# First q and k as fp32 rows by the hardware queue, and an instruction order planned with new transfer rates

## The chip, the cores and the metric

One core of a Trainium2 chip (trn2). The metric is device time in microseconds (us) from the first to the last moment of one execution; medians over several executions are given with their range. A profile has a slightly shorter "span", from the first to the last instruction that it records. The kernel before takes 317.6 us.

## The reference

Sliding-window attention on 8 batches of 8 heads, 576 positions, 64 wide, then a two-layer network on the 4608 resulting tokens:

```python
scores = (1/sqrt(64)) * q @ k.T              # q, k, v: 8 x 8 x 576 x 64, fp32
mask   = (rel >= 0) & (rel < 64)             # rel = query position - key position
attn   = softmax(where(mask, scores, -1e9))
x      = (attn @ v), heads side by side      # 4608 x 512
h      = x @ w_in                            # 512 -> 2048
out    = (h * sigmoid(h)) @ w_out            # 2048 -> 512
```

## The kernel before

The kernel works on bf16 tiles in on-chip memory. Batches 0 to 3 get q (and 0 and 1 get k) by a load that casts fp32 to bf16 in flight, followed by a transpose on TensorE and a copy ("lift") out of its accumulator. Later batches load rows, also cast to bf16 on the way, and have a DMA transpose turn them. v comes in 128-row blocks; VectorE then makes a copy of it that is shifted by 64 partitions (`shift_v`). While TensorE does the two layers for earlier tokens, the attention of the next batch runs between those matmuls. Every exponentiated score tile of batches 1 to 7 is multiplied by the 0/1 mask on VectorE before TensorE may multiply it with v.

No one wrote the order of the instructions by hand. The kernel holds a list scheduler, `Plan`. Each operation is added with the engine it may use, an estimate of its time, what it depends on, and a rank. `run` then plays the whole execution through with these estimates; whenever an engine comes free, it takes the ready operation of best rank. The order that results is emitted, and is fixed from then on: on the chip each engine works through its list in order, whatever the real times are. A transfer has a planned time too:

```python
if op["dma"] is None:
    op["seen"] = end + op["lat"]
else:
    soft = e == "POOL"
    pipe[soft] = max(pipe[soft], pipe[False], end + 0.9) + op["dma"]     # one pipe per kind of queue
    op["seen"] = pipe[soft] + (2.0 if c in ("xk", "xo") else 1.4)        # when it is believed to have landed
```

The parts that the argument touches (cut):

```python
rank=dict(..., exp=1, mask=1, lift=2, spread=2, shift=2, cast=4, ...)    # plus b, the batch: smaller goes first

def load_cast(w, b, pj, kk):                  # q or k of one pair of heads, cast in flight
    nc.gpsimd.dma_start(out=natbs[w]..., in_=(q, k)[kk][b, 2 * pj:2 * pj + 2]...)

def shift_v(b, hf, a, z):                     # copies on VectorE only
    t = vv[b % NK][:, 2 * NB * a:2 * NB * z + 1, 0:D]
    if hf: nc.vector.tensor_copy(out=t[0:64, 2::2], in_=t[64:128, 1::2])
    else:  nc.vector.tensor_copy(out=t[64:128, 0:-1:2], in_=t[0:64, 1::2])

def masking(n, g):
    nc.vector.tensor_mul(es[n % NE], es[n % NE], mask0 if g == 0 else mask)

# planned times of transfers: rows of q, k in later batches 0.6; cast loads 1.0;
# v 1.3; each of the 8 pieces of w_in 1.55, of w_out 1.38
p.add("dma", {"POOL": 1.0}, lambda e, part=part: load_v(e, b, part), busy, dma=1.3)

# matmuls without a use, which fill TensorE's idle time until the first layer is well under way
p.add_filler(60, "warm", {"PE": 0.17}, warm, [*c_bias, c_ident], gate=..., pool="all")
```

The softmax here doesn't subtract the row's maximum and nothing guards it: scores larger than these inputs give would overflow.

## Time and profile before

| | before |
|---|---|
| time | 317.61 us (317.55 to 318.02, 3 runs) |
| TensorE busy | 97% of a span of 315.6 us |
| first layer's first matmul | 24.8 us |
| first transposes | 6.45 us |
| last row of v (batch 7) landed | 188.35 us |

The prediction below shows the lines that carry this. One view is added here, the waits of TensorE. Its columns are what waited, for what, the total in us, how often, and the longest:

```profile
PE at L657 <- DVE bias L191: 3.5, 1, 3.5
PE at L287 <- DMA natb<-in_q_dram: 0.6, 1, 0.6
```

L657 are the warm-up matmuls and L287 are the first transposes. Apart from the start, then, TensorE waits for nobody for longer than a few tenths.

### The profile page before, as it was taken

The page shows a single profiled execution, that of the slowest core. Times are in us where ns is not written, and L with a number is a line of the kernel's source. Part 1 is how long each engine was busy: PE and PEld are TensorE (multiplying, and loading weights), DVE is VectorE, ACT ScalarE, POOL GpSimd, SP SyncE. Part 2 cuts the span into 40 slices and gives each one's busy share as a digit, 9 for nine tenths or more (in the row PEclk, how much of TensorE's full clock was granted, in tenths as well). Part 3 has the DMA queues.
Part 4 walks back from the last instruction along what each step waited for, and adds up shares of the span by engine and source line. Part 5 has one row for each costly group of instructions (what it writes and reads, how often), then busy time and mean ns, then how long its engine had stood idle before and what let it go on. Part 6 is the DMA issues. An engine that isn't in the chain of part 4 may idle for free.

```text
span 315.6 us, 6086 instructions
## 1 busy us (share of the span) xinstructions
PE 307.6 (97%) x2231; PEld 167.7 (53%) x2231; DVE 152.8 (48%) x465; ACT 194.1 (61%) x381; POOL 120.8 (38%) x161
## 2 busy tenths in 40 slices
PE   5899999999999999999999999999999999999995
PEld 2668666545655456545654565455444444444444
DVE  5691858854788638895895089606800000000000
ACT  8798795787848687467618762777176136316611
POOL 8965958876748642867645400000000000000000
PEclk9999999999999999999999999999999999999999
DMA  7999999999999999999999995302320110020011
GB/s 68 173 194 189 158 200 167 154 226 160 144 152 158 152 95 159 200 162 132 157 162 188 167 156 119 83 1 56 95 58 2 66 66 2 18 82 33 3 66 66
DMA packets 137309, 37.03 MB, mean 117 GB/s; under 512 B 121664, under 2 KB 132800, under 8 KB 137280
## 3 DMA queue, kind: packets, MB, share of 16 engines
q0 software_dynamic: 96128, 18.36, 78.6%
q1 hardware_dynamic: 41152, 18.29, 31.1%
q8 instruction: 17, 0.28, 0.4%
q14 instruction: 12, 0.10, 0.1%
HBM read 36.70 MB, written 9.44 MB: 146 GB/s over the span
## 4 chain that ended last, share of the span: by engine, by line
PE 92%; DVE 2%; DMA 2%; ACT 1%; POOL 1%; issue 1%; POOLq 0%; ACTq 0%; DVEq 0%
PE mp L428 39%; PE mp L437 39%; PE at L363 5%; PE at L337 5%; DMA natb<-in_q_dram 2%; PE at L296 1%; PE at L419 1%; PE at L287 1%; PE at L657 0%; DVE qbd L309 0%; POOL natb L232 0%; PE mp L657 0%; ACT L355 0%; PE mp L408 0%; POOL vv L260 0%
## 5 line engine op out<-in xcount | busy, mean ns | idle before, releaser
L437 PE MATMUL mp<-w_out_sb,g 128*128 128x512 bf16 (+2 forms) x608 | 145.4, 367 | 0.0
L428 PE MATMUL mp<-bridge,w_in_sb 128*128 128x512 bf16 (+2 forms) x640 | 129.7, 358 | 0.1
L434 ACT ACTIVATE g<-mp 128x512 bf16<-128x512 f32 (+2 forms) x160 | 86.5, 555 | 30.0 <-PE mp L428 29.7
L428 PEld LDWEIGHTS <-w_in_sb 128*128 128x128 bf16 x640 | 60.4, 98 | 59.6 <-issue 0.4
L437 PEld LDWEIGHTS <-g 128*128 128x128 bf16 x608 | 54.4, 97 | 41.3
L443 ACT COPY ot<-mp 128x512 f32<-128x512 f32 (+2 forms) x36 | 20.1, 563 | 73.7 <-PE mp L437 56.8
L392 DVE TENSOR_TENSOR ox<-at,rc 64x192 bf16<-64x192 f32 x120 | 42.4, 354 | 2.6
L242 POOL DMA_DIRECT2D nat<-in_k_dram x48 | 36.1, 754 | 17.1 <-DMA vv<-in_v_dram 7.0
L260 POOL DMA_DIRECT2D vv<-in_v_dram x32 | 32.0, 1002 | 24.8 <-PE at L363 15.5
L355 ACT ACTIVATE e<-at 128x384 bf16<-128x384 f32 x89 | 37.9, 498 | 2.1 <-PE at L337 1.9
L358 DVE TENSOR_TENSOR e<-e,mask 128x384 bf16<-128x384 bf16 x84 | 26.5, 346 | 24.5 <-ACT e L355 23.8
L363 PEld LDWEIGHTS <-e 128*128 128x128 bf16 x288 | 22.6, 96 | 15.2 <-DVE e L358 2.1
L363 PE MATMUL at<-vv,e 128*128 128x130 bf16 x273 | 29.8, 219 | 0.0
L242 POOL DMA_DIRECT2D nat<-in_q_dram x32 | 24.3, 764 | 7.9 <-DMA nat<-in_q_dram 4.7
L337 PE MATMUL at<-qbd,kt 128*128 128x128 bf16 x252 | 22.8, 219 | 0.2
L337 PEld LDWEIGHTS <-kt 128*128 128x128 bf16 x252 | 17.8, 98 | 9.6 <-issue 1.4
L369 DVE RECIPROCAL rc<-at 128x6 f32<-128x6 f32 x91 | 17.3, 194 | 10.0 <-PE at L363 8.2
L302 DVE COPY qbd<-at 64x288 bf16<-64x288 bf16 x25 | 12.0, 479 | 16.0 <-ACT qbd L302 14.4
L375 DVE TENSOR_TENSOR ob<-at,rc 64x192 bf16<-64x192 f32 x48 | 16.8, 350 | 0.9
L256 DVE COPY qbd<-raw 64x1152 bf16<-64x1152 bf16 x16 | 7.9, 497 | 13.2 <-DMA raw<-nat 12.9
L302 ACT COPY qbd<-at 64x288 bf16<-64x288 bf16 x23 | 11.0, 478 | 2.9 <-DVE qbd L302 1.9
L232 POOL DMA_DIRECT2D natb<-in_q_dram x16 | 10.7, 670 | 4.8 <-PE mp L428 1.3
(66 smaller groups left out, 160.9 us busy)
## 6 DMA issues: line engine op xcount, KB each, us to landing
out_dram<-ot SPq DMA_DIRECT2D x35, 256.0 KB, 2.5
vv<-in_v_dram POOLq DMA_DIRECT2D x32, 144.0 KB, 6.9
nat<-in_k_dram POOLq DMA_DIRECT2D x48, 72.0 KB, 8.0
natb<-in_q_dram POOLq DMA_DIRECT2D x16, 144.0 KB, 6.3
nat<-in_q_dram POOLq DMA_DIRECT2D x32, 72.0 KB, 8.1
w_in_sb<-in_moe_w_in_dram POOLq DMA_DIRECT2D x8, 256.0 KB, 8.4
w_out_sb<-in_moe_w_out_dram POOLq DMA_DIRECT2D x8, 256.0 KB, 8.3
natb<-in_k_dram POOLq DMA_DIRECT2D x8, 144.0 KB, 5.9
```

The costliest lines, as they stand in the source:

```text
L242: nc.gpsimd.dma_start(out=rows(i)[:, pj % 2, :, 64 * hh:64 * hh + 64], in_=(q, k)[kk][b, 2 * pj + hh].rearrange("(m p) d -> p m d", p=NR),)
L260: queue[e].dma_start(out=vv[b % NK][:, 2 * g0 + 1:2 * g1 + 1:2, 0:D], in_=v[b].rearrange("h s d -> (h s) d").rearrange("(g p) d -> p g d", ...
L302: copies[e](out=qbd[b % NK][64 * hh:64 * hh + 64, pj, hh].rearrange("x (p m) -> x p m", m=NM)[:, :, r::2], in_=at_bf16(op)[64 * r:64 * r + ...
L337: nc.tensor.matmul(at_sp(op)[:, x], lhsT=kt[b % NK][:, pj * S + t * 64:pj * S + t * 64 + 128], rhs=qbd[b % NK][:, pj, :, t * 64:t * 64 + 6 ...
L355: nc.scalar.activation(out=es[n % NE], in_=at_sp(op), func=ACTF.Exp, scale=scale)
L358: nc.vector.tensor_mul(es[n % NE], es[n % NE], mask0 if g == 0 else mask)
L363: nc.tensor.matmul(at_pv(op)[:, x], lhsT=es[n % NE][:, x].rearrange("p h i -> p (h i)"), rhs=vv[b % NK][:, s:s + NB + 1:NB, 0:D + 1], star ...
L392: nc.vector.tensor_mul(ox(n)[:, :, r], pv[r, :, hh, 0:D], rc[r, :, hh:hh + 1].to_broadcast([64, 3, 64]))
L428: nc.tensor.matmul(banks[bank["bank"]][:, lo:hi], lhsT=w_in_sb[:, c, ft * 128:(ft + 1) * 128], rhs=bridge[:, (j * TT + lo) // 64:(j * TT + ...
L434: nc.scalar.activation(out=gts[gt][:, lo:hi], in_=banks[bank["bank"]][:, lo:hi], func=ACTF.Silu)
L437: nc.tensor.matmul(banks[bank["bank"]][:, 0:hi - lo], lhsT=gts[gt][:, m * 128:(m + 1) * 128], rhs=w_out_sb[:, f, lo:hi], start=(f == 0), s ...
L443: copies[e](out=ots[ot][:, lo:hi], in_=banks[bank["bank"]][:, 0:hi - lo])
```

## The change

The intent has two parts. (1) The first pair's q and k no longer wait behind GpSimd's cast loads: SyncE loads them as fp32 rows, and VectorE or ScalarE cast them. (2) The planned times of transfers are replaced by rates measured on batch 1 and on the weights, so that the plan resembles the chip more closely. The planned time of the identity constant is corrected along with them (0.5 to 1.3).

```diff
-    c_ident = p.add("one", {"POOL": 0.5}, const_ident)
+    c_ident = p.add("one", {"POOL": 1.3}, const_ident)
...
+    def load_first(i, kk):                      # fp32 rows, hardware queue
+        nc.sync.dma_start(out=nats[i]....bitcast(FP32)..., in_=(q, k)[kk][0, 0:2]...)
+    def cast_first(e, i, w):
+        copies[e](out=natbs[w], in_=nats[i]....bitcast(FP32))
...
+                if (b, pj) == (0, 0):
+                    ld = p.add("ld0", {"SP": 0.45 if kk else 1.2}, ... load_first(i, kk), dma=1.15)
+                    ca = [p.add("cast", {"ACT": 0.84, "DVE": 0.56}, ... cast_first(e, i, w), [ld], b=b)]
+                else:
-                ca = [p.add("dma", {"POOL": 0.66}, ... load_cast(w, b, pj, kk), ..., dma=1.0)]
+                    ca = [p.add("dma", {"POOL": 0.66}, ... load_cast(w, b, pj, kk), ..., dma=0.85 if b else 1.0)]
...
-    p.add("dma", {"POOL": 1.0}, ... load_v(e, b, part), busy, dma=1.3)
+    p.add("dma", {"POOL": 1.0}, ... load_v(e, b, part), busy, dma=1.1 if b else 1.3)
...
-    win.append(p.add("dma", {"POOL": 0.8}, ... load_w_in(f), dma=1.55))
+    win.append(p.add("dma", {"POOL": 0.8}, ... load_w_in(f), dma=1.35))
...
-    wout.append(p.add("dma", {"POOL": 0.8}, ... load_w_out(f), dma=1.38))
+    wout.append(p.add("dma", {"POOL": 0.8}, ... load_w_out(f), dma=1.28))
```

The four `dma=` edits change no transfer. They change only what the planner believes, and through that the order of everything.

More of the change, by code (lines that the diff above doesn't have):

```diff
@@ L235, in load_cast @@
         )
+    def load_first(i, kk):
+        nc.sync.dma_start(
+            out=nats[i].rearrange("p j m x -> p (j m x)").bitcast(FP32).rearrange("p (h y) -> p h y", h=2),
+            in_=(q, k)[kk][0, 0:2].rearrange("h (p m) d -> p h (m d)", m=NM),
+        )
+    def cast_first(e, i, w):
+        copies[e](out=natbs[w], in_=nats[i].rearrange("p j m x -> p (j m x)").bitcast(FP32))
     def rows(i):
@@ L507, in add_batch_qk @@
                 n_nat[1] += 1
-                ca = [p.add("dma", {"POOL": 0.66}, lambda _, w=w, pj=pj, kk=kk: load_cast(w, b, pj, kk),
-                            [natb_free.get(w)] + (v_landed[b - 1] if b > 2 else []), dma=1.0)]
+                if (b, pj) == (0, 0):
+                    i = n_nat[0] % NN
+                    n_nat[0] += 1
+                    ld = p.add("ld0", {"SP": 0.45 if kk else 1.2}, lambda _, i=i, kk=kk: load_first(i, kk), dma=1.15)
+                    ca = [p.add("cast", {"ACT": 0.84, "DVE": 0.56}, lambda e, i=i, w=w: cast_first(e, i, w), [ld], b=b)]
+                    nat_free[i] = ca[0]
+                else:
+                    ca = [p.add("dma", {"POOL": 0.66}, lambda _, w=w, pj=pj, kk=kk: load_cast(w, b, pj, kk),
+                                [natb_free.get(w)] + (v_landed[b - 1] if b > 2 else []), dma=0.85 if b else 1.0)]
                 by = {"ACT": 0.64, "DVE": 0.75}
@@ L535, in add_v_loads @@
         v_landed.setdefault(b, []).extend(
-            p.add("dma", {"POOL": 1.0}, lambda e, part=part: load_v(e, b, part), busy, dma=1.3) for part in parts)
+            p.add("dma", {"POOL": 1.0}, lambda e, part=part: load_v(e, b, part), busy, dma=1.1 if b else 1.3) for part in parts)
     def add_batch_v(b):
@@ L662 @@
     for f in range(8):
-        win.append(p.add("dma", {"POOL": 0.8}, lambda _, f=f: load_w_in(f), dma=1.55))
+        win.append(p.add("dma", {"POOL": 0.8}, lambda _, f=f: load_w_in(f), dma=1.35))
     add_batch_attention(0)
@@ L670 @@
             for f in range(8):
-                wout.append(p.add("dma", {"POOL": 0.8}, lambda _, f=f: load_w_out(f), dma=1.38))
+                wout.append(p.add("dma", {"POOL": 0.8}, lambda _, f=f: load_w_out(f), dma=1.28))
         while TB * (n_tile + 1) <= b * NB:
```

## The prediction

> **What bounds the kernel now.** I read the page first, for the engine that is never idle. The first line of its busy table and two of the slice rows say which:
>
> ```profile
> PE 307.6 (97%) x2231; PEld 167.7 (53%) x2231; DVE 152.8 (48%) x465; ACT 194.1 (61%) x381; POOL 120.8 (38%) x161
> PE   5899999999999999999999999999999999999995
> DMA  7999999999999999999999995302320110020011
> ```
>
> TensorE works from the second slice on, so the time is (the moment its useful work gets going) + (a nearly fixed amount of work) + (gaps). Next I read the chain of waits in order of time (start, length, what) to find that moment:
>
> ```profile
> 1.51 0.77 POOL natb L232
> 3.09 0.65 POOL natb L232
> 3.74 1.02 POOL vv L260
> 4.75 5.51 DMA natb<-in_q_dram
> 10.31 0.57 PE at L287 x12
> ...
> 15.14 0.53 DVE ox L398
> 24.86 1.43 PE mp L428 x16
> 26.29 0.81 PE at L657 x5
> 27.10 4.37 PE mp L428 x51
> ```
>
> The chain starts with GpSimd issuing loads one after another, then waits 5.5 us for the second pair's q, and reaches the first layer (L428) at 24.8 us. From there it is TensorE to the end: 315.6 - 24.8 = 290.8 us. L657 are warm-up matmuls without a use, so "busy" before 24.8 us is partly padding. Then the windows (PE, PEld, DVE, ACT, POOL busy) of the attention of batch 0:
>
> ```profile
> 5.00:10.00 5.00, 4.72 (x46) 2.52 (x44) 1.40 (x4) 3.53 (x6) 5.00 (x7) 1.00 1.41 136
> 15.00:20.00 5.00, 4.81 (x80) 3.46 (x78) 4.85 (x16) 4.38 (x13) 3.65 (x5) 1.00 1.48 193
> ```
>
> Until 10 us VectorE and ScalarE starve (1.40 and 3.53 of 5 us); at 15 to 20 us both are nearly full (4.85 and 4.38). So the start of the first layer is bound by data first and by these two engines afterwards. Last, the timeline of the beginning:
>
> ```profile
> 1.49 0.79 POOL L232 DMA_DIRECT2D natb<-in_q_dram  x1 [0.18 <-issue]
> 2.03 4.66 ACT L212 COPY qbd<-zero 64x1152 f32<-64x1152 f32 x4
> 3.53 1.44 PE L657 MATMUL at<-bias,ident 128*128 128x384 bf16 x4 [3.53 <-DVE bias L191]
> 3.73 1.02 POOL L260 DMA_DIRECT2D vv<-in_v_dram  x1
> 6.45 0.56 PE L287 MATMUL at<-ident,natb 96*64 96x96 bf16 x12
> 7.93 0.32 DVE L325 COPY vv<-vv 64x576 bf16<-64x576 bf16 x1 [0.25 <-DMA vv<-in_v_dram]
> 10.31 0.56 PE L287 MATMUL at<-ident,natb 96*64 96x96 bf16 x12 [0.59 <-DMA natb<-in_q_dram]
> ```
>
> The trace's landings: q0 4.84, k0 6.63, v0 7.91, q1 10.27, v3 (last of batch 0) 16.95, w_in's last chunk 28.6, batch 1's q0 29.34 us. The first transposes (6.45) begin 1.6 us after q0 landed: they stand behind nine warm-up matmuls in TensorE's order. Only q1 is truly waited for.
>
> **What the Trainium skill says.** (1) "DMA: Bandwidth & Descriptors", section "SWDGE vs HWDGE vs iDMA": a cast in flight needs GpSimd's software descriptors, a plain copy may go by SyncE's hardware ones. So rows by the hardware queue must come as fp32 and be cast by an engine, as the change does. The trace agrees in kind: all loads are in the software queue. (2) The same page, "Latency and other measured facts": DMA engines 7 and 15 are usually slower, a matter of the software path. The landings agree in number: of q1's 16 completions 14 came by 8.96 us and two at 10.06 and 10.27; two stay about 1.2 us behind all through batch 0. The trace doesn't name the engines. (3) "TensorE: Matmul & The Clock Gate", Part 1: about 3.4 us of activity, in a free-running window, before the full clock. The warm-up matmuls here start 0.32 us apart until 6.04 us and 0.16 us apart after 6.9: a little under 3 us. (4) "ScalarE: Activation LUTs" gives 186 ns + 0.833 ns per element with immediate operands; L212's 1152 elements take 4.66/4 = 1.165 us against 1.146, so it holds.
>
> **The change part by part.**
>
> Removed: two cast loads, q0 and k0, from GpSimd: 0.79 + 0.65 = 1.44 us of its issue time. The build's order shows v0 now right after the masks' constants; from 3.73 us it moves to about 2.25. All later loads follow by the same order, so the stream moves by about 1.45 us: q1 lands near 8.8, v3 near 15.5, w_in's last near 27.1, batch 1's q0 near 27.9. This is an estimate; the fp32 rows share the DMA engines at the start, when those are still empty (33 GB/s in the first 5 us).
>
> Added: two fp32 transfers of 288 KB on SyncE, issued from about 0.75 us. Stores of 256 KB on this queue land in 2.5 us, so I expect q0 by about 3.5 and k0 by about 4.5 us. Two casts of 96x768: ScalarE by the formula 186 + 0.833 x 768 = 0.83 us; VectorE about 0.5 (a v shift of 576 elements takes 0.32 us; by length 0.43). Neither starts at landing. VectorE comes to its cast after its constants, near 5.0 us (they end at 5.01 now), giving 5.5. ScalarE comes to k's cast after the four clears: 2.03 + 4.66 = 6.69, plus 0.83 = 7.52 us.
>
> Moved: the order puts 14 warm-up matmuls ahead of the first transposes, nine before. They start with bias, 0.5 us earlier (3.0), and are still at half rate: 10 x 0.32 + 4 x 0.16 = 3.85, so q0's transposes come at about 6.9 instead of 6.45. k0's: after four more, 7.95 instead of 7.70; its lift on ScalarE at 8.45 instead of 8.18. The order then has q1's transposes before the first scores, so these fall from 8.73 to about 9.6 us. The first pair is thus not earlier at all, although its data is. What is earlier is the second pair: q1's transposes at about 9.1 (10.31), and its first scores at about 11.9 (12.84): 0.9 us gained.
>
> From there VectorE and ScalarE decide. Over 5 to 25 us their busy times sum, less the clears' 1.69, to about 28.2 us from 6.7 on, in 2 x 18.1 us: 78% used. The change adds 0.83 there (k's cast; q's lies in idle time): 29.0 us. At the same 78% the first layer would start 0.5 us later; at 85%, 29.0/(2 x 0.85) = 17.1, so at 23.8; at 90% at 22.8. The starvation between 8.6 and 10.9 us (VectorE idle 2.26 us before its second q lift) is what goes, so I take 84 to 85%: first layer at 23.9, gain 0.9 us.
>
> After that: in the old trace TensorE loses 0.47 us at 42.8 to 43.5, where batch 1's scores wait for the last lifts of k. In the new order the last transposes of batch 1 stand eight groups of first-layer matmuls ahead of those scores (one to two before), so this goes. But batch 1's first transposes stand after about 11 groups of tile 0 instead of 17: 23.9 + 4.6 = 28.5 us, against a landing at 27.9. Only 0.6 us of slack, where it was 1.9. I count -0.35 us for this stage. The later tiles have about 1.7 us of gaps above the steady cadence in all; re-planned, I count zero.
>
> Sum: -0.9 - 0.35 = -1.25; 317.61 - 1.25 = 316.3 us.
>
> **The rivals.** (a) The loads stay the bound: if the fp32 rows hold up the software stream, or two lagging engines lag more, TensorE stalls at batch 1's transposes and the gain is that of the stream only, 0 to 0.5 us: 317.2. For it: DMA is at 9 tenths from the second slice. Against: the stream's total is the same and it starts into idle engines. (b) The full data gain: utilization reaches 90% and the first layer starts at 22.8, gaps go too: 315.2. Against it: 4.85 of 5 us on VectorE already. (c) Nothing, or a loss: 14 slow warm-ups and the ScalarE cast behind the clears make the first pair late, VectorE and ScalarE carry 1.3 us more work, and the sum eats the gain: 317.6 to 318. For it: the half-rate clock is in the trace. (d) New gaps in later batches, since the whole order is made anew: half a microsecond either way.
>
> **Range and chances.** 2% is 6.4 us. All that lies before the first layer is 24.8 us, of which VectorE and ScalarE need over 14 each; no path reaches 6.4 us of gain, and a loss of that size would need a stall that no view hints at. So within 2% almost surely: 0.98. Within it, (b) and (c) set the edges: 314.9 to 317.7 us.
>
> **What would show it.** Right: the first L437 (the first layer's new line) at 23 to 24.8 us; q0's transposes no earlier than 6.45 though its rows land before 5; no wait of TensorE for q1; v3 landing 1.2 to 1.7 us earlier; no wait for k's lift near 42 us. Wrong: a first layer before 22.5 (VectorE and ScalarE weren't the bound) or after 24.8; TensorE waiting for batch 1's q or for w_in; rows landing after 5 (q) or 6.7 (k); or a change after 65 us larger than that before it.

## The result, and the profile after

The changed kernel takes **326.30 us** (325.40 to 326.87, 6 runs) where the kernel before takes 317.58 us (316.68 to 318.02, 6 runs beside it). The ratio is 1.0276, with a 95% interval of 1.0254 to 1.0298: slower. Here and below a ratio is the mean time of one kernel's runs over that of the other's runs of the same rounds, so it is not quite the ratio of the medians quoted. Executions over 1.5% slower than the fastest of the same kernel are left out of the means.

The page of the changed kernel shows where to look before any detail does. These are its busy table and two of its slice rows:

```profile
PE 310.1 (95%) x2234; PEld 169.2 (52%) x2234; DVE 157.6 (48%) x474; ACT 192.2 (59%) x372; POOL 120.0 (37%) x159
PE   5999999999999999999999469999999999999996
PEclk9999999999999999999999959999999999999999
```

TensorE's row, unbroken before, has a hole in slices 23 and 24 (each is 8.1 us), and the clock row has its only dip in the second of them. The waits of TensorE name the hole:

```profile
PE at L372 <- DVE e L367: 7.2, 1, 7.2
PE at L673 <- DVE bias L191: 3.3, 1, 3.3
```

L372 multiplies masked scores with v ("values") and L367 is the mask. One wait of 7.2 us for one mask appears where there was none. Why was the mask late? The chain of waits around it, in order of time (start, length, what), answers:

```profile
177.29 10.12 DMA vv<-in_v_dram
...
187.53 0.76 DVE vv L334
...
188.30 0.76 DVE vv L332
...
189.07 0.46 DVE qbd L265
...
189.56 0.37 DVE e L367
...
189.98 0.51 PE at L372 x3
```

The last load of v was issued at 177.29 and landed at 187.41 us. The two shift copies of it ran (L334, L332), then a spread of q (L265), then the mask, then TensorE. But this v belongs to batch 7, and the mask and the values matmul belong to batch 6: they need nothing of it. VectorE's own timeline, after, shows the link (in brackets the idle time before, and what ended it):

```profile
179.25 0.45 DVE L265 COPY qbd<-raw 64x1152 bf16<-64x1152 bf16 x1 [9.42 <-DMA raw<-nat]
187.53 0.76 DVE L334 COPY vv<-vv 64x2304 bf16<-64x2304 bf16 x1 [7.84 <-DMA vv<-in_v_dram]
188.30 0.76 DVE L332 COPY vv<-vv 64x2304 bf16<-64x2304 bf16 x1
189.07 0.46 DVE L265 COPY qbd<-raw 64x1152 bf16<-64x1152 bf16 x1
189.56 0.63 DVE L367 TENSOR_TENSOR e<-e,mask 128x384 bf16<-128x384 bf16 x2
```

And before:

```profile
180.84 0.92 DVE L256 COPY qbd<-raw 64x1152 bf16<-64x1152 bf16 x2 [10.75 <-DMA raw<-nat]
182.09 0.74 DVE L358 TENSOR_TENSOR e<-e,mask 128x384 bf16<-128x384 bf16 x2 [0.33 <-ACT e L355]
...
197.93 0.76 DVE L325 COPY vv<-vv 64x2304 bf16<-64x2304 bf16 x1
```

Read the two together. Before, the masks came at 182.09 and the shift of batch 7's v at 197.93, with no wait: the v had landed at 188.35, long before. After, the same shift stands ahead of the masks, and VectorE sits idle for 7.84 us in front of it, although v landed 0.9 us *earlier* than before. Nothing here became slower. A copy that had been behind the masks now stands in front of them, in a list that is worked off in order. The Trainium skill ("TensorE: Matmul & The Clock Gate", section "Architectural detail: the array is 16× 32×32, not 1× 128×128") says that ScalarE and VectorE are strict FIFO; the trace agrees: VectorE idles for 7.84 us until 187.53, although ScalarE had begun the mask's first input (a row of exponentials, L364) at 181.44 and all five of that row were done by 183.46.

There is a second part. The windows give busy time of PE, PEld, DVE, ACT and POOL, then TensorE's granted clock. After:

```profile
185.00:190.00 5.00, 0.02 (x1) 0.03 (x2) 2.41 (x5) 0.00 (x0) 0.00 (x0) 0.77 0.77 101
190.00:195.00 5.00, 5.00 (x27) 3.10 (x28) 3.04 (x11) 1.71 (x4) 0.00 (x0) 0.55 0.00 0
```

Before:

```profile
190.00:195.00 5.00, 5.00 (x36) 2.71 (x35) 4.55 (x17) 1.81 (x4) 0.00 (x0) 1.00 0.42 95
```

After the pause TensorE runs "fully busy" at a clock of 0.55. In the trace, matmuls of 512 columns then start 0.43 us apart instead of 0.216, until about 194.5 us. The clock record has half the clock from 187.7 to 194.5 us, 6.8 us in all, the first 2.3 of them while TensorE still waits. The same page of the skill (Part 1, "What's actually happening") has the rule: after an idle window of about 3.4 us the clock is halved, until a sustained busy window. The trace agrees in kind: half rate for 4.5 us of work after a gap of 7.40 us (counted from when the next matmul would have started at the steady spacing). So the pause is paid for twice: 7.4 us of gap and 2.2 us from slow matmuls, 9.6 us together. The spans differ by 325.0 - 315.6 = 9.4 us. By these sums one wait is the whole loss; e1 and e2 below test it.

Why did the planner move the shift? Its own times, which it computes when the kernel is built, can be printed and laid beside the trace (in us from the start):

| batch 7 | before: plan | before: chip | after: plan | after: chip |
|---|---|---|---|---|
| last load of v issued | 177.06 | 177.81 | 170.19 | 177.29 |
| last load of v landed | 187.09 | 188.35 | 177.51 | 187.41 |
| first of the two shift copies | 198.12 | 197.93 | 177.51 | 187.53 |
| batch 6's next mask | 182.08 | 182.09 | 181.78 | 189.56 |

With the old numbers the plan was right to about a microsecond at 180 us. With the "measured" ones it believes that v lands at 177.51, 9.9 us too early. Of these, 7.1 us are there when the last load is issued (170.19 against 177.29), because GpSimd waits for earlier landings before it issues (11.8 us in all from 150 to 178 us, in the trace after); the rest is the flight itself. It sees VectorE free at 177.51, no mask ready before 181.78, and a shift that may go: by its rules it takes the shift. On the chip that slot is a trap.

The rates were measured on batch 1, and there they are right: in the trace after, batch 1's q and k land about 0.7 us after the load ahead of them, and v about 1.0. Late in the kernel the same loads share the DMA engines with DMA transposes and stores: in the packets of the trace before, the loads' queue (software) moves 191 GB/s from 20 to 28 us while the other queue (hardware: transposes and stores) moves none; from 161 to 181 us it moves 59 GB/s beside 115. Batch 7's sixteen row loads then landed from 161.35 to 181.00, 1.31 us apart where the plan said 0.6; its four v loads came (188.35 - 181.00)/4 = 1.84 us apart where the plan said 1.3 and now says 1.1. The old 1.3, 1.0, 1.55 and 1.38 were too slow for batch 1; taken together they made good, by luck, for rows planned twice too fast. That the sharing is what slows the loads fits these numbers, but no run took the transposes or the stores away.

The start, where the prediction had looked for the whole effect, moved little:

| | before | after | predicted |
|---|---|---|---|
| q, k of the first pair landed | 4.84, 6.63 | 3.86, 4.77 | 3.5, 4.5 |
| first transposes | 6.45 | 7.38 | 6.9 |
| second pair's q landed | 10.27 | 7.31 | 8.8 |
| last v of batch 0 landed | 16.95 | 14.82 | 15.5 |
| last piece of w_in landed | 28.6 | 26.59 | 27.1 |
| first layer's first matmul | 24.80 | 25.20 | 23.9 |

The timeline of the start, after:

```profile
3.30 1.44 PE L673 MATMUL at<-bias,ident 128*128 128x384 bf16 x4 [3.30 <-DVE bias L191]
...
4.69 0.55 DVE L244 CAST natb<-nat 96x768 bf16<-96x768 f32 x1
...
6.60 0.83 ACT L244 CAST natb<-nat 96x768 bf16<-96x768 f32 x1
...
7.38 0.56 PE L296 MATMUL mp<-ident,natb 96*64 96x96 bf16 x12
```

q is cast at 5.24 us, yet its transposes start at 7.38: fourteen warm-up matmuls (L673) stand before them, from 3.30 on, and take 4.08 us (most start 0.32 us apart), where the plan counts 0.17 us each, 2.4 us. k's cast waits for ScalarE's clears until 6.60. The data came earlier; the order did not let it be used.

### The profile page after: what moved, and what is told of

It is laid out like the page before. It is cut to its first block, busy times and chain, and to the rows that moved or that the text cites. A ratio compares the mean times of both kernels' runs of the same rounds, so it can differ in the third digit from the quotient of the medians.

```text
span 325.0 us, 6088 instructions
## 1 busy us (share of the span) xinstructions
PE 310.1 (95%) x2234; PEld 169.2 (52%) x2234; DVE 157.6 (48%) x474; ACT 192.2 (59%) x372; POOL 120.0 (37%) x159
## 4 chain that ended last, share of the span: by engine, by line
PE 88%; DVE 6%; DMA 3%; issue 1%; ACT 0%; POOL 0%; POOLq 0%; DVEq 0%; ACTq 0%
PE mp L446 36%; PE mp L437 36%; PE at L372 5%; PE at L346 4%; DMA vv<-in_v_dram 3%; DVE ox L401 1%; PE at L673 1%; DVE qbd L318 1%; PE at L305 1%; DVE vv L332 1%; PE mp L673 1%; PE at L296 1%; PE at L428 1%; DVE vv L334 1%; DVE rc L378 0%
## 5 line engine op out<-in xcount | busy, mean ns | idle before, releaser
L446 PEld LDWEIGHTS <-g 128*128 128x128 bf16 x608 | 55.2, 98 | 43.2
L452 ACT COPY ot<-mp 128x512 f32<-128x512 f32 (+2 forms) x34 | 18.9, 560 | 70.5 <-PE mp L446 59.5
L364 ACT ACTIVATE e<-at 128x384 bf16<-128x384 f32 x89 | 38.2, 498 | 14.2 <-PE at L346 13.4
L367 DVE TENSOR_TENSOR e<-e,mask 128x384 bf16<-128x384 bf16 x84 | 26.4, 348 | 28.9 <-ACT e L364 28.1
L269 POOL DMA_DIRECT2D vv<-in_v_dram x32 | 32.7, 1027 | 13.8 <-DVE ob L384 7.9
L372 PE MATMUL at<-vv,e 128*128 128x130 bf16 x273 | 30.4, 222 | 7.5 <-DVE e L367 7.2
L372 PEld LDWEIGHTS <-e 128*128 128x128 bf16 x288 | 22.9, 98 | 24.2 <-DVE e L367 9.8
L311 DVE COPY qbd<-at 64x288 bf16<-64x288 bf16 x28 | 13.4, 479 | 8.0 <-ACT g L443 4.6
L334 DVE COPY vv<-vv 64x576 bf16<-64x576 bf16 (+1 forms) x14 | 7.5, 534 | 11.9 <-DMA vv<-in_v_dram 11.6
L265 DVE COPY qbd<-raw 64x1152 bf16<-64x1152 bf16 x16 | 8.0, 499 | 9.7 <-DMA raw<-nat 9.4
```

The costliest lines, as they stand in the source:

```text
L269: queue[e].dma_start(out=vv[b % NK][:, 2 * g0 + 1:2 * g1 + 1:2, 0:D], in_=v[b].rearrange("h s d -> (h s) d").rearrange("(g p) d -> p g d", ...
L364: nc.scalar.activation(out=es[n % NE], in_=at_sp(op), func=ACTF.Exp, scale=scale)
L372: nc.tensor.matmul(at_pv(op)[:, x], lhsT=es[n % NE][:, x].rearrange("p h i -> p (h i)"), rhs=vv[b % NK][:, s:s + NB + 1:NB, 0:D + 1], star ...
L446: nc.tensor.matmul(banks[bank["bank"]][:, 0:hi - lo], lhsT=gts[gt][:, m * 128:(m + 1) * 128], rhs=w_out_sb[:, f, lo:hi], start=(f == 0), s ...
L452: copies[e](out=ots[ot][:, lo:hi], in_=banks[bank["bank"]][:, 0:hi - lo])
```

## The experiments

Eleven runs, in three groups, each group on one chip beside eleven runs of the kernel before (medians 317.61, 317.79, 317.29 us).

**Theory P (place in the order):** the loss is the shift of batch 7 ahead of batch 6's masks, put there by the plan. **Rivals:** R, the fp32 rows or the casts disturb later transfers, and the wait is only where it shows; and S, the new order costs in many small places. The first four runs separate them: two move the shift and nothing else on purpose, two split the change. The expectations use other letters: A is theory P; B (late transfers) and C (a spread loss, or the fp32 rows) are what R and S stand for here. From e6 on, theory D says that the start is late because the first pair's transposes stand behind warm-ups, theory E that VectorE's and ScalarE's work sets it whatever the first pair does.

### e1: the shift planned late, all else as in the changed kernel

```diff
-  load_v(e, b, part), busy, dma=1.1 if b else 1.3)
+  load_v(e, b, part), busy, dma=3.0 if b == 7 else 1.1 if b else 1.3)
```

The number is only what the planner believes of batch 7's v; no transfer is changed. In a listing of VectorE's order made at build, in which the two halves of one operation share a row, the two copies move 39 and 40 rows down, behind the masks. Nothing before them changes, and the orders of ScalarE, GpSimd and SyncE are the same throughout.

> The changed kernel with one planning number altered: the last batch's v loads are planned at 3.0 us each, so the two copies that shift that batch's v stand 39 rows later in VectorE's order, behind batch 6's masks; loads, casts and every duration are as in the changed kernel. Theory A (head of line: VectorE idles 7.8 us on a copy that nobody needs yet, and the clock drops for about 5 us after): the wait of TensorE near 182 us and the half-rate stretch go, 326.3 - 7.4 - 2.2 = 316.7 us, between 316 and 317.5. Rival B (the late transfers themselves are too late, and TensorE would wait for them wherever the copy stands): still 323 or more. Rival C (the loss is spread, from the fp32 rows or the new order): between 320 and 326.

Measured: five of six runs took 316.75 to 318.59 us; ratio 1.0001 (0.9976 to 1.0026). The loss is gone. The sixth run, which happened to be the profiled one, took 651.75 us; it isn't compared with anything. Its busy table is worth one look:

```profile
PE 643.5 (99%) x2234; PEld 268.9 (41%) x2234; DVE 159.9 (25%) x474; ACT 199.0 (31%) x372; POOL 119.0 (18%) x159
```

VectorE's and ScalarE's work is nearly what it is elsewhere (157.6 and 192.2 us in the changed kernel), while TensorE takes about double: warm-ups start 0.39 us apart, and from 90 us on most 512-column matmuls 0.44 us apart instead of 0.216. So the profile of this kernel had to be taken again (e5).

### e2: the shift planned early, all else as in the kernel before

```diff
-  load_v(e, b, part), busy, dma=1.3)
+  load_v(e, b, part), busy, dma=-0.8 if b == 7 else 1.3)
```

A negative time is nonsense as a rate, but does what is wanted: it makes the plan believe in an early landing. No fp32 rows, no new rates. GpSimd's order stays the same, and so does VectorE's up to the masks.

> The kernel before with one planning number altered: the last batch's v loads are planned as nearly free, so its two shifting copies stand directly ahead of batch 6's masks in VectorE's order, as in the changed kernel; no fp32 rows, no other rate touched. Theory A: VectorE idles until the v rows land near 188 us, TensorE waits about 7 us and then runs some 5 us at half rate: 325 to 328 us. Rivals B and C (the change's transfers or fp32 rows are to blame): within 1 us of 317.6.

Measured: 327.32 us (326.33 to 327.79, 4 runs), ratio 1.0301 (1.0275 to 1.0326). VectorE's timeline:

```profile
181.11 0.92 DVE L256 COPY qbd<-raw 64x1152 bf16<-64x1152 bf16 x2 [10.10 <-DMA raw<-nat]
189.40 0.75 DVE L325 COPY vv<-vv 64x2304 bf16<-64x2304 bf16 x1 [7.36 <-DMA vv<-in_v_dram]
190.16 0.76 DVE L323 COPY vv<-vv 64x2304 bf16<-64x2304 bf16 x1
190.95 1.16 DVE L358 TENSOR_TENSOR e<-e,mask 128x384 bf16<-128x384 bf16 x4
```

The kernel before, with two copies in another place, shows the same picture and the same loss: TensorE's wait is 7.1 us. Rival R has nothing left to explain.

### e3 and e4: the change in halves

e3 is the changed kernel with the four old rates:

```diff
-  dma=0.85 if b else 1.0    /  dma=1.1 if b else 1.3  /  dma=1.35  /  dma=1.28
+  dma=1.0                   /  dma=1.3                /  dma=1.55  /  dma=1.38
```

e4 is the kernel before with the four new ones, and without the rows.

> The changed kernel with all four planned rates of the kernel before (1.0, 1.3, 1.55, 1.38): only the fp32 rows, their casts and the planned time of the identity constant remain. The build puts the last shift at row 338, behind batch 6's masks. Theory A: no late wait, 316.5 to 318.5. Rival C (the fp32 rows cost it): 322 or more. The first layer starts near 25.3 us as in the changed kernel, if the start is set by the 14 warm-up matmuls and the casts.

> The kernel before with the four new planned rates alone, no fp32 rows. The build puts the first of the two last shifting copies two masks behind the place it has in the changed kernel, ahead of batch 6's first reciprocals. Theory A: the rates alone make the loss, somewhat smaller as two masks pass first: VectorE idle 4 to 6 us, TensorE 3 to 6 us, in all 320 to 325. Rival: the fp32 rows are needed for the loss: within 1.5 us of 317.6.

Measured: e3 317.36 us (316.92 to 318.0, 4 runs), ratio 0.9993 (0.9968 to 1.0017): the rows alone are worth nothing, with the first layer at 25.53 us and the first transposes as late as 7.87. e4 324.61 us (324.26 to 325.77, 4 runs), ratio 1.0229 (1.0199 to 1.0259): the rates alone bring most of the loss (slower beyond doubt; whether by 2% is unclear). In e4 VectorE's order has one shift copy after two of the masks, and the timeline shows it:

```profile
182.61 0.74 DVE L358 TENSOR_TENSOR e<-e,mask 128x384 bf16<-128x384 bf16 x2 [0.66 <-ACT e L355]
188.34 0.76 DVE L325 COPY vv<-vv 64x2304 bf16<-64x2304 bf16 x1 [4.99 <-DMA vv<-in_v_dram]
```

TensorE's waits in e4:

```profile
PE at L363 <- DVE e L358: 4.3, 1, 4.3
...
PE at L296 <- DMA natb<-in_q_dram: 1.2, 1, 1.2
```

The gap is 4.4 us instead of 7.40, half rate costs about 2.3 us again, and a wait of 1.2 us for a cast load near 71 us comes on top: 7.9 us, against a difference in span of 322.8 - 315.6 = 7.2; small gaps elsewhere shrank by about as much as is left over. What remains of rival S is that 1.2 us. The experiment also says how touchy the plan is: the same rates put one copy or two ahead of most of the masks, depending on what else is in the plan. In builds that weren't run, putting back only one of the rates of v, of the cast loads or of w_in left both copies early; putting back only that of w_out left one early.

### e5: e1 once more, for its profile

> The kernel of e1_late_shift once more, for a profile in the fast state: the profiled execution of e1 fell into one where every matmul ran at half rate throughout (650 us) and is no use for comparing. Theory A expects a span near 315.8 us, no wait over 0.5 us of TensorE near 182 us, VectorE's shift after the last v landed, and the first layer at 25.3 us as in the changed kernel.

Measured: 317.38 us in a single run (so its state is unknown, but the time is that of e1's fast runs), span 315.6, equal to the kernel before. VectorE:

```profile
180.15 0.92 DVE L265 COPY qbd<-raw 64x1152 bf16<-64x1152 bf16 x2 [10.27 <-DMA raw<-nat]
182.22 0.74 DVE L367 TENSOR_TENSOR e<-e,mask 128x384 bf16<-128x384 bf16 x2 [1.15 <-ACT e L364]
...
198.07 0.76 DVE L334 COPY vv<-vv 64x2304 bf16<-64x2304 bf16 x1
```

Masks at 182.22, shift at 198.07 without a wait: the picture of the kernel before. Theory P stands: moving the copies alone brings the loss (e2), moving them back alone takes all of it away (e1).

This leaves the second question. Without its accident the change is worth nothing, where 1.25 us of gain had been predicted. The first layer starts at 25.23 us in e5. Is the start bound by VectorE's and ScalarE's work, as the prediction had it, or held up by the order?

### e6: fewer warm-ups ahead of the first transposes

e1's kernel, with one more edit:

```diff
-    p.add_filler(60, "warm", {"PE": 0.17}, ...
+    p.add_filler(60, "warm", {"PE": 0.32}, ...
```

0.32 us is what a warm-up takes at half rate in the trace. The plan then puts 7 of them ahead of the first transposes instead of 14, and gives both casts to VectorE.

> The kernel of e1 with the warm-up matmul planned at its measured cold 0.32 us instead of 0.17: seven of them stand ahead of the first transposes, not 14, and the plan gives both casts to VectorE. Theory D (the start is late because the first pair's transposes stand behind warm-ups): q's transposes at about 5.7 us instead of 7.4, first scores near 8.5 instead of 10.2, the first layer 0.6 to 1.5 us earlier (23.8 to 24.7), the time 0.5 to 1.5 us under e1: 316.3. Theory E (VectorE's and ScalarE's work from there on sets the start, whatever the first pair does): first layer within 0.4 us of 25.3, the time within 0.4 us of e1.

Measured: 315.53 us (314.62 to 316.46, 6 runs), ratio 0.993 (0.991 to 0.995). The start:

```profile
4.69 1.47 DVE L244 CAST natb<-nat 96x768 bf16<-96x768 f32 x2
...
5.63 0.45 PE L296 MATMUL mp<-ident,natb 96*64 96x96 bf16 x3
...
22.55 0.58 PE L437 MATMUL mp<-bridge,w_in_sb 128*128 128x192 bf16 x5
```

The first transposes come right after the first cast, 1.75 us earlier than in the changed kernel, and the first layer 2.7 us earlier. Not all of that is gain: in this order the first groups of the first layer start before the last attention work of batch 0 has gone through, so the mark is a flattering one. The span is 2.0 us shorter than e5's.

### e7 and e8: clears out of the way as well, with and without the rows

e7 adds to e6 that ScalarE's clears for batch 1's q may not be planned before 9 us, and have their measured times, so that k's cast and the lifts don't stand behind them. e8 puts the same two edits of the start into the kernel before (old rates, no rows).

```diff
-  c_q = {i: [p.add("first", {"ACT": 1.0}, ... clear_q(i, hh), [c_zero])
+  c_q = {i: [p.add("clear" if i else "first", {"ACT": 1.17 if i or hh else 3.2}, ... clear_q(i, hh), [c_zero],
+                   gate=(lambda: p.now > 9.0) if i else None)
```

> As e6, and ScalarE's clears of batch 1's q tiles (two of 1.17 us) moved behind the first lifts, so ScalarE is free at about 4.4 us instead of 6.7. Theory D: the first lifts start about 1 us earlier than in e6, the first layer at 23 to 24 us, the time 315 to 316.3. Theory E: the clears are work that has to be done somewhere before 25 us, so nothing is gained over e6.

> The kernel before with the same two edits of the start (warm-ups planned at 0.32 us, batch 1's clears later), without fp32 rows and with its old rates. It tells what the fp32 rows are worth once the start isn't held up: q lands at 4.84 and k at 6.63 by the software queue, and q of the second pair at 10.3. If the rows matter: 317 to 317.6, 1 us or more over e7. If not: within 0.4 us of e7.

Measured: e7 317.1 us (316.38 to 317.68, 6 runs), ratio 0.998 (0.996 to 0.9999), first layer at 24.68 us. e8 317.08 us (316.59 to 317.51, 6 runs), ratio 0.998 (0.9964 to 0.9995), first layer at 24.72 us. Moving the clears takes back most of what fewer warm-ups gave. The clears had filled time in which ScalarE had nothing to do (in e7 it is idle for 2.0 us before 6.35); moved, they run at 10.29 and 13.23, and from 10 to 15 us ScalarE is busy 4.94 of 5 us in e7 against 4.52 in e6. That this is the cause is argued from the trace: the re-planned order differs in other places too. e7 and e8 are equal, so with these edits of the start the rows are worth nothing, as in e3.

### e9, e10, e11: what the warm-ups, the rows and the rates are worth

e9 is the kernel before with only the warm-ups planned at 0.32. e10 is the changed kernel with that and with the four old rates, so it has the rows and the warm-ups. e11 is the changed kernel with the warm-ups at 0.32 and with rates for late batches read from the trace instead of batch 1's:

```diff
-  load_rows(i, b, pj, kk, hh), ..., dma=0.6)
+  load_rows(i, b, pj, kk, hh), ..., dma=1.0 if b > 3 else 0.6)
-  load_v(e, b, part), busy, dma=1.1 if b else 1.3)
+  load_v(e, b, part), busy, dma=1.8 if b > 3 else 1.1 if b else 1.3)
```

> The kernel before with only the warm-up matmul planned at 0.32 us (five ahead of the first transposes, nine before). If the start of e6 comes from the warm-ups alone, this is near e6: 315.2 to 316.3, first layer 22.5 to 23.5. If the fp32 rows carry it (second pair's q at 7.3 instead of 10.3): 316.8 to 317.8, first layer 24 to 25.

> e6 with the four planned rates of the kernel before: fp32 rows and fewer warm-ups only. It tells what the new rates are worth when the last shift stands late in both. If they are worth the late lifts of batch 1: 0.4 to 1 us over e6, 316 to 316.6, with a wait for lifts near 42 us. If nothing: 315.2 to 315.9.

> The changed kernel with the warm-up at 0.32 us and, instead of one number for one batch, rates for batches 4 to 7 that come from the trace: 1.8 us for a v load, 1.0 for a row load. The shift of the last v then stands behind the masks by itself. Theory A and D: as e6, 315.0 to 316.0; a new order of the late batches may cost or give 0.3 us.

| | time (range, runs) | ratio (95%) | first layer |
|---|---|---|---|
| e9, warm-ups only | 316.31 (315.78 to 316.70, 5) | 0.9962 (0.9947 to 0.9977) | 24.03 |
| e10, rows and warm-ups | 315.31 (314.27 to 315.71, 6) | 0.9929 (0.9913 to 0.9944) | 21.48 |
| e11, rows, warm-ups, late rates | 315.98 (314.40 to 317.42, 6) | 0.9958 (0.9930 to 0.9985) | 22.20 |

e9 and e10 ran on the same chip beside the same runs of the kernel before, and their intervals just miss each other: the warm-ups alone bring 1.0 us, and the rows (with the identity's planned time) 1.0 us more once the warm-ups no longer hold them up. e10 has the lowest ratio, and it needs none of the new rates; e6, which has them (with the late shift), is as fast: 0.993 on another chip.

e11 shows that rates read from the late batches cure the accident: the shift stands behind the masks without being forced there. Fewer warm-ups are not what does it: in a build that wasn't run, with them but without the late rates, one copy stays early, and with the late rates alone both stand late. The late rates bring no more time than that. e11's median is 0.7 us above e10's, but the intervals overlap; a new wait, for a cast load near 69 us, is the likely reason:

```profile
PE at L305 <- DMA natb<-in_q_dram: 1.3, 1, 1.3
```

And e10 isn't free of the late wait either:

```profile
PE at L372 <- DVE e L367: 0.8, 1, 0.8
```

That is a mask again, at 179.5 to 180.7 us, and with it about a microsecond that a better order could still win.

## Why the prediction was wrong

- **The step that failed** is the term "The later tiles have about 1.7 us of gaps above the steady cadence in all; re-planned, I count zero", with rival (d), "half a microsecond either way", and "a loss of that size would need a stall that no view hints at". The term was wrong in mechanism and not only in size: the new order had a wait in it. It measured +9.6 us: 7.4 us of gap and 2.2 us of half rate. The sum of the gaps that an order has says nothing of the gaps that another order will have. A view did hint at it: the comparison of the two orders, which was at hand, has batch 7's shift in VectorE's list ahead of batch 6's masks, and the trace before has that v landing at 188.35 us, 6.3 us after the first of those masks ran. The prediction used the comparison only for the start and for the stretch near 42 us. Two of the signs of being wrong that it had named did appear: a first layer after 24.8 us, and a change after 65 us larger than that before it.
- **The loads** went as predicted or better: every landing in the table of the start is within 0.7 us of its number except the second pair's q, which came 1.5 us sooner. Rival (a) did not happen.
- **The casts** were right: 0.83 us on ScalarE as the formula gave, 0.55 us on VectorE for "about 0.5"; ScalarE came to k at 6.60 for 6.69 predicted.
- **The first transposes** "no earlier than 6.45" was right in kind. They came at 7.38 instead of 6.9, because the warm-ups started at 3.30 instead of 3.0 and more of them ran at half rate.
- **"84 to 85%: first layer at 23.9, gain 0.9 us"** was wrong in sign: 25.20 us, a loss of 0.4. The test is the utilisation itself. From 6.7 us to the first layer VectorE was busy 15.39 and ScalarE 13.73 of 18.5 us: 29.12/37.0 = 79%. Before it was 13.97 + 13.89 of 2 x 18.1: 77%. The work came in sum as predicted (29.0), but the utilisation rose by 2 points instead of 7, so the start carried the added work at nearly the old rate; the prediction's own line for 78%, 0.5 us later, is close to what happened. Rival (c) had this right: late first pair, more work, no gain. e6 and e10 show that the two engines' capacity was not the limit: with another order at the start they reach 82% and 87% and a shorter time (though some attention work of batch 0 then falls behind the mark). That the warm-ups are what held the order up rests on e9 and e10; e6 moves a cast to VectorE as well.
- **The stall at 42.8 to 43.5 us** went, as predicted: the gaps between 40 and 45 us fell from 0.57 to 0.1 us or less. TensorE never waited for batch 1's q.
- Start +0.4, this stall -0.5, late wait +9.6: +9.5 us, against 9.4 measured in span. Without the late wait the change is worth nothing (e1 1.0001, e3 0.9993), so even the small gain predicted, 1.25 us, wasn't there.
- Two slips without weight: before, the first scores start at 8.90 us (at 8.73 there is a warm-up), and 317.61 - 1.25 is 316.36.

## What to carry to other kernels

An order that was fixed at build is only as good as its model at every point of the run, so a rate measured in one stage must not be given unchecked to stages with other traffic. When a planner's numbers change, compare the orders of every in-order engine to the very end, and ask of each instruction that waits for a transfer: what stands behind it, and when did that transfer land in the old trace? And earlier data is worth only what the instructions queued before its use let through: here the rows brought nothing (e3) while a filler planned at half its real time stood before their use, and 1.0 us (e10 against e9) when it didn't.

## What the Trainium skill lacked or had wrong

- "TensorE: Matmul & The Clock Gate", Part 1: the rule for the halved clock held in kind, and made one wait cost 2.2 us more. An idle window of about 3.4 us is more than it took: in e4 the clock record turns to half at 187.4 us, 2.2 us after TensorE's last matmul made way (185.2), and 2.3 us were lost after a gap of 4.4. The page has no figure for how long the half clock lasts after such a gap inside a dense kernel; in both kernels the record has 6.8 us, twice that window, of which 4.5 us (4.6 in e4) fell on work.
- The same page warns that the clock's records can be unreliable. Here one execution of about a hundred ran its matmuls at half rate or a little less for nearly all of its 650 us (e1), with the summary giving a clock of 1.00 and the slice row missing; the page's own case is another, a clock stuck at a quarter for "50+µs". TensorE's busy time (643.5 us for work that takes 310) tells it, the clock record doesn't.
- "DMA: Bandwidth & Descriptors" gives bandwidths of copies and of DMA transposes, each by itself. It has no rate for loads that share the engines with transposes and stores: v loads that landed 1.0 us after the load ahead in batch 1 landed 1.84 us apart in batch 7, and row loads 1.31 us apart.
